# A planned attention and GLU kernel: half-gate Tanh kept in its partitions, |Q| of the first heads by a VectorE bit mask, and another table of scheduling rules

## The chip, the core and the metric

The kernel runs on one core of a Trainium2 chip. The metric is device time in microseconds (us) of one execution; lower is better. In the profile PE is TensorE, ACT is ScalarE, DVE is VectorE, POOL is GpSimd, and SP is the SyncE queue that issues nearly all DMAs. PSUM is the memory that matmuls write; a bank of it holds 128 partitions x 512 float32 values.

## The reference, cut to what matters

Everything is bfloat16 at the borders, with S = 2048 tokens, D = 640, H = 32 heads of Dh = 20, and F = 1728.

```python
xn = layernorm(x)
q, k, v = split(xn @ wqkv)                    # 32 heads of 20
p = softmax(q @ k.T * 20 ** -0.5)             # 2048 x 2048 per head
s = (p @ v) @ wo
h = sigmoid(xn @ w_gate) * (xn @ w_up)        # 2048 x 1728
g = silu(h @ w_down)
out = x + s * g
```

The heaviest part is the softmax: 32 heads x 2048 x 2048 exponentials.

## The kernel before

**Tiles.** Four heads form a group, 512 queries form a chunk: 8 groups x 4 chunks make 32 blocks. A block has 64 score tiles (4 heads x 16 key tiles), each 128 keys x 512 queries, made by one matmul (`score_mm`, L931). There are 2048 score tiles in all.

**Two ways to an exponential.** A score tile goes one of two ways. On ACT an Exp turns it into bfloat16 (`pt`, all through the helper at L142): two tiles at once, 128 x 1024, from a PSUM pair `scA`, and sometimes a third tile, 128 x 512, from a single bank `bk`. On DVE the tile is read out of a bank as int16 (`iv`, L1310), and four such tiles together go through three more passes (`passes`: L1019, L1022 and L1025) that build the exponential from the bits (`pb`). PE then multiplies `pt` and `pb` by V and sums the result in one bank (L967).

**A bound on the scores.** Instead of a running maximum the kernel subtracts a bound. For it the absolute value of Q is needed in bfloat16. For the first two groups (heads 0 to 7, `mk_q`) five matmuls make Q in a bank, ACT writes `aq` = |Q| (`q_abs`, L232), one matmul adds the bound to the same bank (L236), and DVE writes `q` (L239). The first block does this in the prologue, so seven such items are left for the main part. For the other heads (`mk_qu`) Q goes to SBUF first, and DVE makes |Q| there by masking the sign bit (L611).

**The GLU.** The sigmoid is computed as Tanh: h is made as (1 + tanh(g/2)) * u, and the halves are made good later. For each chunk of 512 tokens there are 13 full tiles of 128 hidden columns: gate matmuls, Tanh on ACT to `tnh`, up matmuls, and one DVE instruction (L716) to `hT`. The last 64 hidden columns share one matmul output: the gate is in partitions 0 to 63, the up part in partitions 64 to 127 (`mm2`, L720). There `th2` writes the Tanh of partitions 0 to 63 to partitions 64 to 127 of `tnh`, and `ev2` (L728) multiplies it with the up part and writes partitions 0 to 63 of `hT`. There are four such half tiles, one per chunk. The down projection follows (`mk_down`, L746), with a Tanh of its own on ACT (`td`) and a DVE instruction at L762; its result goes to DRAM (`gq_dram`) and comes back later.

**The end.** In the last eight blocks the output projection (`mk_out`, L805) is made tile by tile: DVE multiplies it with the gate (`otmp`, L812), POOL adds x (L815), SP stores the tile (L817). A tile of x and of the gate is loaded by `load_out` (L787, L788) into one of two places, so tile t can be loaded only after tile t-2 is done with its place.

**What sets the order.** The order of PE, ACT and DVE is not left to a scheduler of the compiler. The kernel contains a planner: while it builds the program it steps through an imagined time of its own, with a cost for each operation (for example 0.60 us for a DVE read of a bank), and at each step emits the next instruction of an engine that it holds to be free. On PE it chooses between filling score tiles (`F`), multiplying by V (`PV`) and the other matmuls (`M`). ACT takes fills in turn, DVE takes bank reads, passes and the items above. On the chip each engine runs its list in order, and semaphores keep the data right; the planner's time then has no meaning.

**The table.** The planner's choices hang on some 18 numbers, and `PLAN` has a row of them for each of the 32 blocks; a row comes into force when its block is begun (L1188). Among them are `s0` and `s1` (how far ahead DVE may be given score tiles), `rounds` (how many products with V must be ready), `mfew` (how many banks other items may take), `third`, `excl` and `lag`. The constant `D_LAST` (20) in `claim_dve` says with how many tiles left a block gives DVE no more of them:

```python
if n_left[b] >= (D_LAST if b < NBLK - 1 else D_LAST_END):
    js = [j for j in range(GH) if left[b][j] and j not in not_j]
    return take(b, max(js, key=lambda j: (j not in had, len(left[b][j]), j)), -1) if js else None
```

Of the kernel before, what the change touches and what calls it, by code (L numbers as in the profile page):

```python
# [11 lines left out]
BF16 = mybir.dt.bfloat16  # L12
I16 = mybir.dt.int16
ACT = mybir.ActivationFunctionType
ALU = mybir.AluOpType
# [3 lines left out]
P = 128  # L19
# [5 lines left out]
QC = 512  # L25
# [3 lines left out]
UC = UH * DH  # L29

B_PV = (3, 2, 1, 0)
LEAD, D_LAST, D_LAST_END, M_END = 40.0, 20, 8, 0.6
NPT, NPB, NIV = (21, 7), 4, 3
A_BANKS = (((), ()), ((0,), (1,)), ((0, 1, 2, 3), (1, 0, 2, 3)))
D_BANKS = ((2, 1, 0, 3), (2, 0, 1, 3), (0, 1, 2, 3), (1, 2, 0, 3))
M_BANKS = ((3, 2, 1, 0), (2, 3, 0, 1), (3, 1, 2, 0), (3, 0, 2, 1))

RULE = dict(urgent=0.25, rounds=4, hold=0.15, slack=0.2, s0=0.2, s1=0.2, wait3=0.4, fall=1, lag=0.0,
            dmax=2, third=2, dord=0, mord=0, mfew=2, npv=4, held=48, burst=1, excl=1)
KEYS = tuple(RULE)  # L40
PLAN = (
    (0.25, 4, 0.3, 0.2, 0.2, 0.2, 0.4, 1, 0.0, 2, 0, 0, 2, 2, 4, 48, 1, 1),
    (0.25, 4, 0.3, 0.2, 0.2, 0.5, 0.4, 1, 0.0, 2, 0, 0, 1, 2, 3, 48, 1, 1),
    (0.25, 4, 0.15, 0.2, 0.5, 0.2, 0.4, 1, 0.0, 2, 2, 0, 0, 2, 4, 48, 1, 1),
    (0.25, 2, 0, 0.2, 0.2, 0.5, 0, 1, 0.0, 2, 2, 0, 0, 2, 4, 48, 1, 1),
    (0.25, 4, 0.15, 0.2, 0.8, 0.2, 0.4, 1, 0.0, 2, 2, 0, 0, 2, 4, 40, 1, 1),
    (0.25, 4, 0.15, 0.2, 0.8, 1.2, 0.4, 1, 0.0, 2, 2, 0, 0, 1, 4, 40, 1, 1),
    (0.25, 4, 0.15, 0.5, 0.8, 1.2, 0.4, 1, 0.0, 2, 2, 0, 3, 1, 4, 32, 1, 1),
    (0.25, 2, 0.15, 0.5, 0.8, 0.8, 0.4, 1, 0.0, 2, 2, 0, 3, 1, 4, 32, 1, 1),
    (0.25, 2, 0.15, 0.5, 0.5, 0.8, 0.4, 1, 0.0, 2, 2, 0, 2, 1, 4, 32, 0, 1),  # L50
    (0.25, 2, 0.15, 0.5, 0.5, 0.8, 0.4, 1, 0.0, 2, 2, 0, 2, 1, 4, 32, 0, 1),
    (0.25, 2, 0.15, 0.5, 0.5, 1.2, 0.4, 1, 4.0, 2, 2, 0, 2, 1, 4, 56, 0, 1),
    (0.3, 2, 0.15, 0.5, 0.5, 1.2, 0.4, 1, 4.0, 2, 2, 3, 2, 1, 4, 56, 0, 1),
    (0.25, 4, 0.15, 0.2, 0.2, 0.8, 0.4, 1, 0.0, 2, 2, 0, 0, 1, 4, 64, 1, 1),
    (0.25, 4, 0.15, 0.2, 0.2, 1.2, 0.4, 1, 0.0, 2, 2, 0, 0, 2, 4, 48, 1, 1),
    (0.25, 4, 0.3, 0, 0.2, 1.2, 0.2, 1, 0.0, 2, 2, 0, 0, 2, 4, 48, 1, 1),
    (0.25, 4, 0.3, 0, 0.8, 1.2, 0.2, 1, 0.0, 2, 2, 0, 0, 2, 4, 48, 1, 1),
    (0.25, 4, 0.3, 0, 0.5, 1.2, 0.2, 1, 0.0, 2, 2, 0, 0, 1, 4, 48, 1, 1),
    (0.25, 4, 0.15, 0.2, 0.8, 0.2, 0.4, 1, 0.0, 2, 2, 2, 1, 2, 4, 48, 1, 1),
    (0.25, 4, 0.15, 0.2, 0.8, 0.2, 0.4, 1, 0.0, 2, 2, 2, 1, 2, 4, 48, 1, 1),  # L60
    (0.25, 4, 0.15, 0.2, 0.35, 0.2, 0.4, 1, 14.0, 2, 2, 0, 0, 2, 4, 48, 1, 1),
    (0.2, 4, 0.15, 0.2, 0.2, 0.8, 0.7, 1, 0.0, 2, 2, 0, 0, 2, 4, 48, 0, 1),
    (0.2, 4, 0.15, 0.2, 0.5, 0.8, 0.7, 1, 0.0, 2, 2, 0, 0, 2, 4, 48, 0, 1),
    (0.2, 4, 0, 0.2, 0.5, 0.8, 0.7, 1, 0.0, 2, 2, 0, 0, 2, 4, 48, 1, 1),
    (0.25, 4, 0.3, 0.5, 0.2, 1.2, 0.4, 1, 2.0, 2, 2, 0, 0, 2, 4, 48, 1, 1),
    (0.25, 4, 0.15, 0.2, 0.5, 0.2, 0.4, 1, 0.0, 2, 0, 2, 0, 2, 4, 48, 1, 1),
    (0.25, 4, 0.15, 0.2, 0.5, 0.8, 0.4, 1, 0.0, 2, 0, 2, 0, 2, 4, 32, 1, 1),
    (0.25, 4, 0.15, 0.2, 0.5, 0.2, 0.4, 1, 0.0, 2, 0, 2, 0, 2, 3, 32, 1, 1),
    (0.25, 7, 0.15, 0.2, 0.2, 0.2, 0.2, 1, 0.0, 2, 2, 0, 0, 2, 4, 48, 1, 1),
    (0.2, 7, 0.15, 0.2, 0.2, 0.2, 0.2, 1, 0.0, 2, 2, 0, 0, 2, 4, 48, 1, 1),  # L70
    (0.2, 7, 0.15, 0.2, 0.2, 1.2, 0.2, 1, 0.0, 2, 2, 0, 0, 2, 4, 48, 1, 1),
    (0.2, 7, 0.15, 0.2, 0.2, 0.5, 0.2, 1, 0.0, 2, 2, 0, 0, 2, 4, 48, 1, 1),
    (0.25, 4, 0.15, 0, 0.2, 0, 0.4, 1, 8.0, 2, 2, 0, 0, 2, 3, 48, 1, 1),
)

PRO = (
# [35 lines left out]
def kernel(  # L112
# [11 lines left out]
    nc = tc.nc  # L124
# [14 lines left out]
    def act_imm(o, i, func, scale):  # L139
        zero = mybir.ImmediateValue(dtype=FP32, value=0.0)  # L140
        sc = mybir.ImmediateValue(dtype=FP32, value=scale)
        return nc.scalar.add_instruction(mybir.InstActivation(  # L142
            func=func, name=nc.get_next_instruction_name(), engine=ENG.Activation,
            ins=[nc.scalar.lower_ap(i), zero, sc, zero], outs=[nc.scalar.lower_ap(o)]))
# [7 lines left out]
    wk = ctx.enter_context(tc.tile_pool(name="wk", bufs=2))  # L152
# [77 lines left out]
    def q_abs(ps):  # L230
        aq = wk.tile([P, QC], BF16, tag="aq", bufs=4, name="aq")
        nc.scalar.activation(out=aq, in_=ps, func=ACT.Abs)  # L232
        return aq
# [188 lines left out]
    hT = late.tile([P, NFT, QC], BF16, name="hT")  # L422
# [55 lines left out]
    NBLK = NG * NQC  # L478
# [18 lines left out]
    def mark(*e):  # L497
        return lambda t: ev_at.__setitem__(e, t)
# [33 lines left out]
    def mk_q(b, at):  # L532
        g, c = gc(b)
        st = {}

        def alloc():
            st["ps"] = misc_ps()

        def mm(kd):
            nc.tensor.matmul(st["ps"], lhsT=wslice(g, 0, kd), rhs=xnT[:, c, kd, :],  # L540
                             start=(kd == 0), stop=(kd == KD - 1))

        def ab():
            st["aq"] = q_abs(st["ps"])

        def ev():
            q_evac(st["ps"], qts[b % 3])
        return Item([("PE", alloc, [(T_MM, lambda kd=kd: mm(kd)) for kd in range(KD)]),
                     ("ACT", 0.48, ab),
                     ("PE", None, [(T_MM, lambda: q_bound(st["ps"], g, st["aq"]))]),  # L550
                     ("DVE", 0.60, ev, "free", lambda t: q_at.__setitem__(b, t))], at, pre=[("md", g)])

# [136 lines left out]
    def mk_gu(c, kf, at):  # L689
        st = {}  # L690
        fs = fsz[kf]
        k2, ko = divmod(kf, 2)

        def alloc0():
            if (c, k2) not in wgu_tiles:
                load_wgu(c, k2)
            st["g"] = misc_ps()

        def alloc1():
            st["u"] = misc_ps()  # L700
            if ko == 0:
                n = c * NK2 + k2 + 1
                if n < NQC * NK2:
                    load_wgu(*divmod(n, NK2))

        def mm(key, i, kd):
            w = wgu_tiles[(c, k2)]
            nc.tensor.matmul(st[key][0:fs, :], lhsT=w[:, i, kd, ko * P:ko * P + fs],  # L708
                             rhs=xnT[:, c, kd, :], start=(kd == 0), stop=(kd == KD - 1))

        def th():
            st["t"] = w2.tile([P, QC], BF16, tag="tnh", bufs=2, name="tnh")
            act_imm(st["t"][0:fs, :], st["g"][0:fs, :], ACT.Tanh, 0.5)

        def ev():
            nc.vector.scalar_tensor_tensor(out=hT[0:fs, kf, :], in0=st["t"][0:fs, :], scalar=1.0,  # L716
                                           in1=st["u"][0:fs, :], op0=ALU.add, op1=ALU.mult)

        def mm2(kd):
            nc.tensor.matmul(st["g"], lhsT=wgu_tiles[(c, k2)][:, 0, kd, P:2 * P],  # L720
                             rhs=xnT[:, c, kd, :], start=(kd == 0), stop=(kd == KD - 1))

        def th2():
            st["t"] = w2.tile([P, QC], BF16, tag="tnh", bufs=2, name="tnh")
            act_imm(st["t"][fs:P, :], st["g"][0:fs, :], ACT.Tanh, 0.5)

        def ev2():
            nc.vector.scalar_tensor_tensor(out=hT[0:fs, kf, :], in0=st["t"][fs:P, :], scalar=1.0,  # L728
                                           in1=st["g"][fs:P, :], op0=ALU.add, op1=ALU.mult)
        if fs < P:  # L730
            return [Item([("PE", alloc0, [(T_MM, lambda kd=kd: mm2(kd)) for kd in range(KD)]),
                          ("ACT", 0.48, th2), ("DVE", 0.60, ev2, "free", mark("h", c, kf))], at)]
        return [Item([("PE", alloc0, [(T_MM, lambda kd=kd: mm("g", 0, kd)) for kd in range(KD)]),
                      ("ACT", 0.48, th, "free", mark("t", c, kf))], at),
                Item([("PE", alloc1, [(T_MM, lambda kd=kd: mm("u", 1, kd)) for kd in range(KD)]),
                      ("DVE", 0.60, ev, "free", mark("h", c, kf))], at, gates={1: [("t", c, kf)]})]
# [124 lines left out]
    for b in range(NBLK):  # L861
        g, c = gc(b)
# [58 lines left out]
    def claim_dve(had, not_j):  # L921
        for b in range(base(), min(NBLK, base() + 2)):
            if q_at.get(b, 1e9) > now:
                return None
            if n_left[b] >= (D_LAST if b < NBLK - 1 else D_LAST_END):
                js = [j for j in range(GH) if left[b][j] and j not in not_j]
                return take(b, max(js, key=lambda j: (j not in had, len(left[b][j]), j)), -1) if js else None
        return None
# [592 lines left out]
```

## Time and profile before

| what | value |
|---|---|
| median of 6 runs | 812.03 us (808.84 to 812.68) |
| the profiled execution | 811.98 us |
| its span, first to last instruction | 810.3 us |
| granted TensorE clock, mean | 0.992 |
| busy in the span: ACT, DVE, PE | 782.2, 774.2, 769.1 us |
| first Exp of a score tile starts | 29.55 us |
| last Exp of a score tile ends | 792.97 us |

The busy time is the union of an engine's records. The record of an ACT or DVE instruction begins when the engine takes it up, which can be while the one before is still running; so records overlap, and the distance of two ends tells what an instruction costs in a full queue. In the tables of groups each line has the source line, the engine, the operation, output<-input with shapes, the count, then busy us and mean ns of one, then the engine's idle time before it and what ended it.

### The profile page before, as it was taken

How to read it: one execution, taken by the hardware profiler on the slowest of the kernel's cores; microseconds unless marked ns; L12 is line 12 of the kernel's file. 1: busy time of each engine (PE TensorE's matmuls, PEld its weight loads, DVE VectorE, ACT ScalarE, POOL GpSimd, SP SyncE). 2: the span in 40 equal slices, each digit the busy share in tenths (PEclk: the TensorE clock that was granted, in tenths of full speed). 3: DMA queues.
4: the chain of work that ended last, by engine and by line, in shares of the span. 5: the costliest groups of instructions: out<-in, count | busy, mean ns of one | idle time of the engine just before them, and what ended most of it. 6: DMA issues, size and time to landing. Idle time of an engine off the chain costs nothing.

```text
span 810.3 us, 17151 instructions
## 1 busy us (share of the span) xinstructions
PE 769.1 (95%) x6464; PEld 278.3 (34%) x6516; DVE 774.2 (96%) x1274; ACT 782.2 (97%) x1003; POOL 88.4 (11%) x107
## 2 busy tenths in 40 slices
PE   6899999999999999999999999999999999899985
PEld 5522333333333333334333333334332223333332
DVE  8899999999999999999999999999999999899986
ACT  8899999999999999999999999999999999999992
POOL 7000000010000000000000000000000001212135
PEclk9999999999999999999999999999999999999998
DMA  6611231223122223131112323432122323322431
GB/s 166 174 47 51 64 81 32 79 54 77 52 72 72 61 65 95 51 89 50 56 48 68 96 60 80 121 112 75 48 69 71 85 57 83 114 82 57 141 91 45
DMA packets 95875, 62.61 MB, mean 77 GB/s; under 512 B 36388, under 2 KB 89684, under 8 KB 95792
## 3 DMA queue, kind: packets, MB, share of 16 engines
q1 hardware_dynamic: 95504, 61.18, 27.0%
q8 instruction: 51, 0.84, 0.4%
q10 hardware_dynamic: 288, 0.33, 0.1%
q14 instruction: 32, 0.26, 0.1%
HBM read 47.84 MB, written 13.55 MB: 76 GB/s over the span
## 4 chain that ended last, share of the span: by engine, by line
ACT 57%; PE 25%; DVE 10%; issue 5%; DMA 2%; POOL 1%; SPq 0%; DVEq 0%; ACTq 0%; POOLq 0%
ACT pt L142 51%; PE scA L931 7%; PE bk L708 5%; PE bk L746 5%; PE bk L967 4%; DVE iv L1310 4%; ACT tnh L142 2%; DVE pb L1025 2%; ACT td L142 1%; PE bk L676 1%; POOL xnT L815 1%; DVE pb L1019 1%; DVE pb L1022 1%; ACT sq L338 1%; ACT xnT L362 1%
## 5 line engine op out<-in xcount | busy, mean ns | idle before, releaser
L142 ACT ACTIVATE pt<-scA 128x1024 bf16<-128x1024 f32 x698 | 711.6, 1222 | 3.0 <-PE bk L931 2.7
L1310 DVE TENSOR_SCALAR iv<-bk 128x512 int16<-128x512 f32 x499 | 330.5, 682 | 9.7 <-PE bk L931 7.5
L931 PE MATMUL scA<-q,kT 32*128 32x512 bf16 x1391 | 271.8, 382 | 16.8 <-ACT pt L142 12.6
L931 PE MATMUL bk<-q,kT 32*128 32x512 bf16 x657 | 200.1, 384 | 2.1 <-DVE otmp L812 1.9
L967 PE MATMUL bk<-pt,v 128*21 128x512 bf16 x1549 | 182.6, 382 | 0.0
L931 PEld LDWEIGHTS <-kT 32*128 32x128 bf16 x2048 | 88.1, 91 | 262.8 <-issue 249.7
L967 PE MATMUL bk<-pb,v 128*21 128x512 bf16 x998 | 157.2, 382 | 0.5 <-DVE pb L1025 0.4
L1025 DVE TENSOR_TENSOR pb<-iv,pb 128x2048 bf16<-128x2048 bf16 (+1 forms) x125 | 152.4, 1219 | 0.4
L708 PE MATMUL bk<-xnT,wgu 128*128 128x512 bf16 x488 | 138.4, 382 | 2.3 <-issue 1.3
L142 ACT ACTIVATE pt<-bk 128x512 bf16<-128x512 f32 x158 | 124.6, 789 | 3.2 <-PE bk L931 3.1
L1004 POOL TENSOR_TENSOR on_bf<-on,rl 128x512 bf16<-128x512 f32 x31 | 40.5, 1305 | 646.6 <-DVE rl L1002 581.4
L1019 DVE TENSOR_SCALAR pb<-iv 128x2048 int16<-128x2048 int16 (+1 forms) x125 | 86.8, 694 | 0.4
L1022 DVE TENSOR_SCALAR pb<-iv 128x2048 int16<-128x2048 int16 (+1 forms) x125 | 86.8, 695 | 0.0
L746 PE MATMUL bk<-wd,hT 128*128 128x320 bf16 x448 | 86.2, 306 | 0.6 <-ACT pt L142 0.4
L967 PEld LDWEIGHTS <-v 128*21 128x21 bf16 x2547 | 48.2, 90 | 88.2 <-issue 70.4
L708 PEld LDWEIGHTS <-wgu 128*128 128x128 bf16 x520 | 38.3, 97 | 60.6 <-issue 38.5
L746 PEld LDWEIGHTS <-hT 128*128 128x128 bf16 x448 | 36.4, 98 | 44.8 <-issue 34.7
L568 PE MATMUL bk<-xnT,wu 128*128 128x512 bf16 x151 | 44.4, 382 | 1.4 <-issue 0.5
L142 ACT ACTIVATE tnh<-bk 128x512 bf16<-128x512 f32 (+1 forms) x56 | 44.6, 796 | 0.1
L716 DVE SCALAR_TENSOR_TENSOR hT<-tnh,bk 128x512 bf16<-128x512 bf16 x52 | 35.5, 682 | 2.6 <-ACT tnh L142 0.9
L815 POOL TENSOR_TENSOR xnT<-otmp,xnT 128x320 bf16<-128x320 f32 x24 | 21.9, 924 | 59.6 <-DVE otmp L812 46.9
L676 PE MATMUL bk<-wv,xnT 128*128 128x160 bf16 x280 | 26.6, 234 | 0.2 <-issue 0.2
(116 smaller groups left out, 390.9 us busy)
## 6 DMA issues: line engine op xcount, KB each, us to landing
rl<-rd SPq DMA_DIRECT2D x124, 64.0 KB
wgu<-in_B_w_gate_dram SPq DMA_DIRECT2D x24, 320.0 KB
wgu<-in_B_w_up_dram SPq DMA_DIRECT2D x24, 320.0 KB
gq_dram<-gqs SPq DMA_DIRECT2D x24, 160.0 KB
xnT<-gq_dram SPq DMA_DIRECT2D x12, 320.0 KB
xt<-in_A_x_dram SPq DMA_DIRECT2D x16, 160.0 KB
oD<-on_bf SPq DMA_DIRECT2D x120, 20.0 KB
wd<-in_B_w_down_dram SPq DMA_DIRECT2D x1, 2080.0 KB
```

The lines of the kernel that those rows point to most:

```text
L142: return nc.scalar.add_instruction(mybir.InstActivation(func=func, name=nc.get_next_instruction_name(), engine=ENG.Activation, ins=[nc.sca ...
L568: nc.tensor.matmul(st["ps"], lhsT=wus[u][:, kd, i, :], rhs=xnT[:, c, kd, :], start=(kd == 0), stop=(kd == KD - 1))
L708: nc.tensor.matmul(st[key][0:fs, :], lhsT=w[:, i, kd, ko * P:ko * P + fs], rhs=xnT[:, c, kd, :], start=(kd == 0), stop=(kd == KD - 1))
L716: nc.vector.scalar_tensor_tensor(out=hT[0:fs, kf, :], in0=st["t"][0:fs, :], scalar=1.0, in1=st["u"][0:fs, :], op0=ALU.add, op1=ALU.mult)
L746: nc.tensor.matmul(st["ps"][:, 0:HD], lhsT=hT[0:fsz[kf], kf, t4 * P:(t4 + 1) * P], rhs=wd[0:fsz[kf], kf, h * HD:(h + 1) * HD], start=(kf = ...
L931: nc.tensor.matmul(dst, lhsT=kTs[gc(b)[0] % 2][32 * j:32 * j + 32, kt * P:(kt + 1) * P], rhs=qts[b % 3][32 * j:32 * j + 32, :], start=True ...
L967: nc.tensor.matmul(bank[pv_bank[0]][32 * j:32 * j + DH + 1, :], lhsT=lhsT, rhs=u["src"], start=first, stop=last, tile_position=(0, 32 * j) ...
L1004: nc.gpsimd.tensor_tensor(out=on_bf, in0=on, in1=rl, op=ALU.mult)
L1019: nc.vector.tensor_scalar(out=pb[:, 0, :, :].bitcast(I16), in0=iv, scalar1=0x7F80, scalar2=1, op0=ALU.bitwise_and, op1=ALU.bitwise_or)
L1022: nc.vector.tensor_scalar(out=pb[:, 1, :, :].bitcast(I16), in0=iv, scalar1=0x007F, scalar2=0x3F00, op0=ALU.bitwise_and, op1=ALU.bitwise_or)
L1025: nc.vector.tensor_tensor(out=pb[:, 1, :, :], in0=iv.bitcast(BF16), in1=pb[:, 1, :, :], op=ALU.mult)
L1310: nc.vector.tensor_scalar(out=d["iv"][:, j, :], in0=bank[bk], scalar1=B_OFF, scalar2=0.0, op0=ALU.add, op1=ALU.max)
```

## The change

It has three parts. First, `th2` writes the Tanh of the half gate tile to partitions 0 to 63, where its input lies, and `ev2` reads it from there; its planned cost goes from 0.60 to 0.75. Second, |Q| in `mk_q` is no longer an Abs on ACT: DVE reads the high 16 bits of each float32 in the bank and masks the sign bit. The first block's Abs in the prologue stays on ACT. Third, all rows of `PLAN` are other ones, and the two thresholds of `claim_dve` become columns of the table.

```diff
-LEAD, D_LAST, D_LAST_END, M_END = 40.0, 20, 8, 0.6
+LEAD, M_END = 40.0, 0.6
...
-            dmax=2, third=2, dord=0, mord=0, mfew=2, npv=4, held=48, burst=1, excl=1)
+            dmax=2, third=2, dord=0, mord=0, mfew=2, npv=4, held=48, burst=1, excl=1, dl=20, dle=8)
 KEYS = tuple(RULE)
 PLAN = (
-    (0.25, 4, 0.3, 0.2, 0.2, 0.2, 0.4, 1, 0.0, 2, 0, 0, 2, 2, 4, 48, 1, 1),
-    (0.25, 4, 0.3, 0.2, 0.2, 0.5, 0.4, 1, 0.0, 2, 0, 0, 1, 2, 3, 48, 1, 1),
...
+    (0.25, 4, 0.15, 0.2, 0.8, 0.2, 0.4, 1, 0.0, 2, 2, 0, 0, 2, 4, 48, 0, 1, 20, 8),
+    (0.25, 5, 0.3, 0.2, 0.8, 0.2, 0.4, 1, 0.0, 2, 2, 0, 0, 3, 4, 48, 0, 1, 20, 8),
...
         def ab():
-            st["aq"] = q_abs(st["ps"])
+            st["aq"] = wk.tile([P, QC], BF16, tag="aq", bufs=4, name="aq")
+            high = st["ps"].bitcast(I16).rearrange("p (q h) -> p q h", h=2)[:, :, 1]
+            nc.vector.tensor_scalar(out=st["aq"].bitcast(I16), in0=high, scalar1=0x7FFF, scalar2=0,
+                                    op0=ALU.bitwise_and, op1=ALU.bitwise_or)
...
-                     ("ACT", 0.48, ab),
+                     ("DVE", 0.60, ab),
...
         def th2():
             st["t"] = w2.tile([P, QC], BF16, tag="tnh", bufs=2, name="tnh")
-            act_imm(st["t"][fs:P, :], st["g"][0:fs, :], ACT.Tanh, 0.5)
+            act_imm(st["t"][0:fs, :], st["g"][0:fs, :], ACT.Tanh, 0.5)
 
         def ev2():
-            nc.vector.scalar_tensor_tensor(out=hT[0:fs, kf, :], in0=st["t"][fs:P, :], scalar=1.0,
+            nc.vector.scalar_tensor_tensor(out=hT[0:fs, kf, :], in0=st["t"][0:fs, :], scalar=1.0,
                                            in1=st["g"][fs:P, :], op0=ALU.add, op1=ALU.mult)
...
-                          ("ACT", 0.48, th2), ("DVE", 0.60, ev2, "free", mark("h", c, kf))], at)]
+                          ("ACT", 0.48, th2), ("DVE", 0.75, ev2, "free", mark("h", c, kf))], at)]
...
-            if n_left[b] >= (D_LAST if b < NBLK - 1 else D_LAST_END):
+            if n_left[b] >= (rule["dl"] if b < NBLK - 1 else rule["dle"]):
```

In the instruction order of the changed program the numbers of instructions differ as follows; all other instructions are as many as before, in another order.

| instruction | before | changed |
|---|---|---|
| ACT Exp, 128 x 1024 from `scA` | 693 | 686 |
| ACT Exp, 128 x 512 from `bk` | 158 | 179 |
| ACT Exp, 128 x 512 from `scA` | 5 | 0 |
| ACT Abs, main part | 7 | 0 |
| DVE bit mask from a bank | 0 | 7 |
| DVE `iv`, 128 x 512 | 499 | 497 |
| DVE passes of a last, smaller group (two masks, one product) | 3 of 1536 columns | 3 of 512 columns |
| add of x to an output tile: POOL / DVE | 24 / 0 | 23 / 1 |
| changes of PE between fills, PV and other matmuls | 1428 | 1367 |

## The prediction

> **What bounds the kernel now.** I read the busy shares, then the busy time by stretch, then the tables of groups by shape, then the timeline of ACT and DVE where a stretch shows idle time.
>
> ```profile
> PE 769.1 (95%) x6464; PEld 278.3 (34%) x6516; DVE 774.2 (96%) x1274; ACT 782.2 (97%) x1003; POOL 88.4 (11%) x107
> ...
> 50.00:700.00 650.00, 630.88 (x5254) 215.21 (x5294) 635.80 (x1026) 649.70 (x815) 36.98 (x30) 1.00 0.25 69
> 700.00:716.00 16.00, 14.33 (x104) 5.61 (x102) 12.33 (x22) 13.31 (x19) 6.08 (x6) 0.89 0.55 171
> 775.00:793.00 18.00, 17.14 (x148) 6.47 (x146) 14.60 (x24) 16.27 (x22) 9.13 (x10) 0.94 0.34 102
> ```
>
> After the stretch and its length come PE, weight loads, DVE, ACT and POOL. Three engines look alike in the first line, but from 50 to 700 us ACT is busy 649.70 of 650 us, DVE 635.80. A full record can still hide a wait, because ACT's records overlap, so I looked at their ends:
>
> ```profile
> 522.60 1.35 ACT L142 ACTIVATE pt<-scA 128x1024 bf16<-128x1024 f32 x1
> 523.97 0.59 ACT L142 ACTIVATE tnh<-bk 64x512 bf16<-64x512 f32 x1
> 524.58 2.86 ACT L142 ACTIVATE pt<-scA 128x1024 bf16<-128x1024 f32 x3
> ...
> 685.41 0.60 ACT L142 ACTIVATE pt<-bk 128x512 bf16<-128x512 f32 x1
> 685.90 1.94 ACT L142 ACTIVATE pt<-scA 128x1024 bf16<-128x1024 f32 x2
> ```
>
> The three Exp from 524.58 take 2.86 us; the first, started on an empty engine, takes 1.025 (the line at 708.90 further down is such a one, 1.02), so the next two end (2.86 - 1.025)/2 = 0.917 us apart. At 685.41 a single tile is followed by the next start after 0.49. So in a full queue a 1024-wide Exp costs 0.917 and a 512-wide one 0.490: 0.427 per 512 columns and 0.063 fixed, which makes 0.330 of a 320-wide `td`. The half Tanh at 523.97 starts only when the one before has ended (522.60 + 1.35 = 523.95) and the next starts only when it has ended: end to end 0.61 instead of 0.490, and the next Exp ends 1.05 later instead of 0.917. It costs 0.744 in all.
>
> ```profile
> L142 ACT ACTIVATE pt<-scA 128x1024 bf16<-128x1024 f32 x693 | 709.2, 1225 | 3.0 <-PE bk L931 2.7
> L142 ACT ACTIVATE pt<-bk 128x512 bf16<-128x512 f32 x158 | 124.6, 789 | 3.2 <-PE bk L931 3.1
> L142 ACT ACTIVATE tnh<-bk 128x512 bf16<-128x512 f32 x52 | 42.2, 812 | 0.0
> L232 ACT ACTIVATE aq<-bk 128x512 bf16<-128x512 f32 x7 | 5.5, 791 | 0.0
> L239 DVE TENSOR_SCALAR q<-bk 128x512 bf16<-128x512 f32 x7 | 4.8, 687 | 0.1
> L611 DVE TENSOR_SCALAR aq<-qu 120x512 int16<-120x512 int16 x16 | 4.5, 282 | 0.0
> L728 DVE SCALAR_TENSOR_TENSOR hT<-tnh,bk 64x512 bf16<-64x512 bf16 x4 | 2.8, 690 | 0.6 <-ACT tnh L142 0.3
> ```
>
> ACT's work in the main part: 693 x 0.917 + (158 + 52 + 7 + 5) x 0.490 + 4 x 0.744 + 32 x 0.330 = 635.5 + 108.8 + 3.0 + 10.6 = 757.9 us. From the first Exp (29.55) to the end of the last (792.97) are 763.4 us. So 5.5 us are waiting, and ACT is the bound: 99.3% filled. About 3.1 of the 5.5 lie at 708 to 716, some 2.1 after 775:
>
> ```profile
> 708.41 0.60 ACT L142 ACTIVATE pt<-bk 128x512 bf16<-128x512 f32 x1 [1.55 <-PE bk L931]
> 708.90 1.02 ACT L142 ACTIVATE pt<-scA 128x1024 bf16<-128x1024 f32 x1
> ...
> 706.52 0.89 DVE L812 SCALAR_TENSOR_TENSOR otmp<-bk,xnT 128x320 f32<-128x320 f32 x2 [2.34 <-DMA xnT<-gq_dram]
> ...
> 787.03 1.88 DVE L1310 TENSOR_SCALAR iv<-bk 128x512 int16<-128x512 f32 x3
> ```
>
> At 706.52 DVE stood 2.34 us for a reloaded gate tile; PE then lacked a bank and ACT a fill. The line at 787.03 gives DVE's price: (1.88 - 0.68)/2 = 0.60 per bank read.
>
> **The change part by part.** *Half Tanh.* Writing to its own partitions, ACT has the shape of any 512-wide Tanh: 4 x (0.744 - 0.490) = -1.0 us. For `ev2` the row is L728: 690 ns, and in the timeline it neither overlaps the one before nor the one after. The Trainium skill (VectorE: DVE Perf Modes, "Two Vector instructions with no wait between them") says that an instruction is held until all before have ended when an input starts in another 32-partition quadrant than the last read from that memory. That agrees, and speaks against a gain on DVE: the up part still starts at partition 64 of PSUM, so `ev2` stays held. I take no change; bounds -0.12 x 4 and +0.06 x 4, all on DVE.
>
> *|Q|.* ACT loses 7 x 0.490 = -3.4 us. DVE gains seven masks. By operation the nearest row is L611, 282 ns; by what it reads it is L239, a bank, 687 ns, 0.60 in a queue. The skill's same page ("Why PSUM operands drop a tier") allows a PSUM source two results a cycle at best, and ("What auto-detection actually checks") that needs 16-bit data with step 1; here the step is 2. So 7 x 0.60 = 4.2 us; by L611 it would be about 2. The mask also puts a wait into DVE's queue: for the five Q matmuls, with bank reads queued behind it, and the bound matmul waits for it. The items are made a block ahead (763/32 = 24 us), which hides this; without that cover it is about 7 x 0.6 = 4 us.
>
> *The table: ACT against DVE.* The counts: ACT -7 of 1024, +21 of 512 from banks, -5 of 512 from `scA`: -6.4 + 10.3 - 2.5 = +1.4 us (two tiles more, nine instructions more). ACT in all: -1.0 - 3.4 + 1.4 = -3.0 us, to 754.9. DVE: +4.2, two bank reads less -1.2, the last group's passes narrower. Their rows are 548, 547 and 959 ns at 1536 columns and 696, 695 and 1221 at 2048, so 512 columns should cost about 254, 254 and 435: -1.1. One add moves from POOL (about 0.5, from the 481 ns of L812). In all DVE +2.4. It had 14 us without a record in 50 to 700 alone, so this is not on the path.
>
> *The table: the order.* PE changes 1367 times between kinds of work instead of 1428, with the same matmuls but two; PE is not the bound. Whether ACT keeps filled is what the trace before can't show. Sorting both orders into the work of PE between two fills: over 1.6 us it is 16 times before and 20 times after, largest 1.97 and 2.73 us, against 0.92 to 1.41 us of Exp in one fill and another waiting. That is much alike; I give +0.4 for the one large gap. Before the last fills there is no run of eleven output matmuls any more, where ACT stood 1.2 us at 777: -1.2. Behind the last DVE pass one more `otmp` is left: +0.4. SP issues the same loads and stores. They stand in another order where tiles are reloaded, which is the first rival below. Bounds of the order alone: -5.5 (no wait left) and +10 (below).
>
> Sum: -3.0 + 0.4 - 1.2 + 0.4 = -3.4 us on the profiled 811.98 (span 810.3 and 1.7 around it): 808.6. The median, 812.03, is the same within 0.05.
>
> **The rivals.** *Slower: the reload of output tiles.* DVE's work between freeing a place and using it again is 7.2, 3.6, 27, 28, 12.6, 4.7, 24, 22, 3.8 and 4.1 us before, for tiles 2 to 11; after it is 4.1, 6.6, 36, 39, 4.1, 3.8, 21, 23, 8.4 and 5.6. At 3.6 DVE stood 2.34 us and ACT lost 3.1; there SP issued the load only at 703.4, behind four stores of `oD`, a load of `lt` and a store of `out` that held SP for 1.32 us. At 3.8, 4.1 and 4.7 no load was waited for. After the change three stand at 4.1, 4.1 and 3.8. If all three meet a full SP queue: 3 x 3.1 - 3.1 = +6.2, with -3.0 and the tail's +0.4 about 816. It turns slower once two of three wait like that. For: the place is known to stall. Against: one in four did. I give all such ways 0.22.
>
> *The gain is given back.* DVE's share is less even: summing the larger of ACT's, DVE's and PE's work over groups of four blocks gives 777 before and 779 after, where ACT fell by 3. Where DVE leads (the second to fourth blocks: 73.6 us against ACT's 71.1), ACT waits later than before: about +3, so 811.5. Chance 0.16. That the mask costs more than 0.60 ends here too.
>
> *The waits close too.* If the order leaves about 1.5 of 5.5 us of waits: 804.5. Chance 0.14.
>
> **How the numbers follow.** The forecast has 0.48, and its own range is 806.5 to 810.5. A measurement of this kernel tells about 0.3%, 2.4 us, from no change, so faster means under 809.6 and slower over 814.5. Faster: 0.14 and 0.46 of the forecast's, 0.60; within: 0.02 and 0.16, 0.18; slower 0.22. The range 804.0 to 815.5 leaves out about 0.1 at each end.
>
> **What would show it.** Right: ACT from first to last Exp about 760 us with 50 to 700 still full; `tnh` 64x512 without a gap before it and no Exp held behind it; `aq` on DVE at about 0.68 us a record. Wrong: idle ACT released by PE scores after `otmp` waits for `gq_dram`; gaps on ACT where DVE leads; `aq` well over 0.7 us; a first Exp that starts elsewhere than 29.5.

## The result, and the profile after

| | before | changed |
|---|---|---|
| median | 810.11 us (72 runs, 808.45 to 813.25) | 808.13 us (34 runs, 805.91 to 810.96) |
| ratio to before, 95% interval | | 0.9972 (0.9965 to 0.9980) |
| the profiled execution | 811.98 us | 806.70 us |
| its span; granted clock, mean | 810.3 us; 0.992 | 805.0 us; 0.983 |
| first Exp starts, last Exp ends | 29.55, 792.97 us | 30.20, 788.52 us |

The change made the kernel faster by 0.28%, 2.3 us. Measured again beside the experiments, the gain was 0.12% (0.01 to 0.24), so its size is not known well. The six runs of before that the forecast started from were high: with 72 the median is 810.11. So the two profiled executions differ by more (5.3 us) than the medians (2.0): the one of before was 1.9 above its median, the one of the changed kernel 1.4 below. Sizes of single terms are read from the traces in what follows, the worth of a change from the ratios.

The busy shares of the changed kernel and its busy time by stretch (after the stretch and its length: PE, weight loads, DVE, ACT and POOL with their counts, then granted clock, DMA share and GB/s):

```profile
PE 761.7 (95%) x6458; PEld 274.1 (34%) x6514; DVE 778.1 (97%) x1280; ACT 777.7 (97%) x1005; POOL 90.7 (11%) x106
...
50.00:700.00 650.00, 631.80 (x5350) 219.12 (x5397) 639.43 (x1034) 649.46 (x832) 38.31 (x30) 1.00 0.25 70
700.00:716.00 16.00, 15.88 (x139) 5.56 (x139) 15.97 (x29) 15.54 (x18) 4.36 (x5) 1.00 0.53 160
716.00:735.00 19.00, 14.89 (x116) 3.71 (x119) 17.10 (x27) 17.69 (x21) 1.26 (x1) 0.73 0.11 32
...
750.00:766.00 16.00, 13.17 (x96) 3.00 (x95) 14.67 (x23) 14.12 (x16) 5.31 (x5) 0.68 0.55 169
```

ACT is still the bound: 649.46 of 650 us from 50 to 700. DVE grew from 774.2 to 778.1 while ACT fell from 782.2 to 777.7. What is new stands at the end: from 716 to 735 and from 750 to 766 the granted clock is 0.73 and 0.68, ACT has 1.3 and 1.9 us without work, and PE is *less* busy than elsewhere. The groups that the change touches, by shape (count, then busy us and mean ns of one, then idle time before):

```profile
L142 ACT ACTIVATE pt<-scA 128x1024 bf16<-128x1024 f32 x686 | 709.4, 1224 | 5.7 <-PE bk L934 3.4 <-PE scA L934 2.2
L142 ACT ACTIVATE pt<-bk 128x512 bf16<-128x512 f32 x179 | 143.6, 802 | 0.0
L546 DVE TENSOR_SCALAR aq<-bk 128x512 int16<-128x512 int16 x7 | 4.8, 686 | 0.1
L731 DVE SCALAR_TENSOR_TENSOR hT<-tnh,bk 64x512 bf16<-64x512 bf16 x4 | 2.8, 690 | 0.1
L142 ACT ACTIVATE tnh<-bk 64x512 bf16<-64x512 f32 x4 | 2.4, 607 | 0.0
```

The mask takes 686 ns a record, the price of a bank read as forecast, not the 282 of the mask from SBUF. `ev2` keeps its 690 ns.

Three places hold nearly all of ACT's waits. The first, in the timeline (start, duration, engine, line; in brackets the idle time before and what ended it), is the reload of an output tile:

```profile
698.32 0.49 DVE L815 SCALAR_TENSOR_TENSOR otmp<-bk,xnT 128x320 f32<-128x320 f32 x1 [1.10 <-DMA xnT<-gq_dram]
...
698.87 0.37 PE L934 MATMUL bk<-q,kT 32*128 32x512 bf16 x1 [0.79 <-DVE otmp L815]
...
700.46 1.94 ACT L142 ACTIVATE pt<-scA 128x1024 bf16<-128x1024 f32 x2 [0.99 <-PE scA L934]
```

DVE stands 1.10 us for the gate tile, PE then 0.79 for a bank, ACT 0.99 for a fill. The second place is this:

```profile
722.36 0.39 PE L934 MATMUL scA<-q,kT 32*128 32x512 bf16 x2 [0.52 <-ACT pt L142]
...
723.27 0.61 PE L934 MATMUL scA<-q,kT 32*128 32x512 bf16 x2 [0.53 <-ACT pt L142]
...
729.42 1.25 PE L808 MATMUL bk<-xnT,v 128*128 128x320 bf16 x4
...
730.59 0.61 PE L934 MATMUL scA<-q,kT 32*128 32x512 bf16 x2
...
731.30 1.02 ACT L142 ACTIVATE pt<-scA 128x1024 bf16<-128x1024 f32 x1 [0.75 <-PE scA L934]
...
732.75 4.07 ACT L142 ACTIVATE pt<-scA 128x1024 bf16<-128x1024 f32 x4 [0.42 <-PE bk L934]
```

From 719.6 on PE has little but fills: a pair of score matmuls of 0.39 us, then 0.53 us idle until ACT frees the next pair of banks. At 723.27 the same pair takes 0.61: the granted clock had fallen to half at 722.9, and it stayed so for 10.2 us, to 733.2. The fills themselves are still in time. But at 729.42 the other work comes back, four output matmuls take 1.25 us at this clock, the next fill starts at 730.59, and ACT waits. The third place, 759 to 764, is of the same kind: the clock was half from 753.7 to 763.9, and ACT stood 0.44, 0.48 and 0.91 us for score tiles.

Adding up by how much two ends lie further apart than the prices allow, all waits over 80 ns make 5.0 us, where before had 5.8: 1.1 by the reload, 3.9 in the two stretches of half clock. In before the clock was half only for 3.4 us from 708.8 and 3.4 us from 773.7 (an expectation below gives these places as 703 and 768, which is some 6 us too early). Behind the last Exp it is halved in both kernels.

### The profile page after: what moved, and what is told of

Its sections match the earlier page's. It is cut to its first block, busy times and chain, and to the rows that moved or that the text cites. A ratio compares the mean times of both kernels' runs of the same rounds, so it can differ in the third digit from the quotient of the medians.

```text
span 805.0 us, 17176 instructions
## 1 busy us (share of the span) xinstructions
PE 761.7 (95%) x6458; PEld 274.1 (34%) x6514; DVE 778.1 (97%) x1280; ACT 777.7 (97%) x1005; POOL 90.7 (11%) x106
## 4 chain that ended last, share of the span: by engine, by line
ACT 67%; PE 21%; DVE 5%; issue 5%; DMA 1%; POOL 1%; SPq 0%; ACTq 0%; DVEq 0%; POOLq 0%
ACT pt L142 61%; PE scA L934 7%; PE bk L749 5%; PE bk L970 5%; ACT tnh L142 4%; PE bk L711 1%; DVE iv L1313 1%; ACT td L142 1%; PE bk L808 1%; DVE pb L1028 1%; DVE xn L350 0%; ACT xnT L362 0%; PE bk L934 0%; DVE pb L1025 0%; PE bk L841 0%
## 5 line engine op out<-in xcount | busy, mean ns | idle before, releaser
L934 PE MATMUL bk<-q,kT 32*128 32x512 bf16 x676 | 208.3, 387 | 1.3 <-DVE otmp L815 0.8
L934 PEld LDWEIGHTS <-kT 32*128 32x128 bf16 x2048 | 85.4, 91 | 266.3 <-issue 254.8
L970 PE MATMUL bk<-pt,v 128*21 128x512 bf16 x1551 | 175.2, 386 | 0.1
L970 PE MATMUL bk<-pb,v 128*21 128x512 bf16 x994 | 149.5, 386 | 0.0
L142 ACT ACTIVATE pt<-bk 128x512 bf16<-128x512 f32 x179 | 143.6, 802 | 0.0
L749 PE MATMUL bk<-wd,hT 128*128 128x320 bf16 x448 | 84.3, 302 | 0.1
L818 POOL TENSOR_TENSOR xnT<-otmp,xnT 128x320 bf16<-128x320 f32 x23 | 24.2, 1070 | 57.6 <-DVE otmp L815 53.7
```

Of the source, the lines that this page charges most:

```text
L142: return nc.scalar.add_instruction(mybir.InstActivation(func=func, name=nc.get_next_instruction_name(), engine=ENG.Activation, ins=[nc.sca ...
L749: nc.tensor.matmul(st["ps"][:, 0:HD], lhsT=hT[0:fsz[kf], kf, t4 * P:(t4 + 1) * P], rhs=wd[0:fsz[kf], kf, h * HD:(h + 1) * HD], start=(kf = ...
L934: nc.tensor.matmul(dst, lhsT=kTs[gc(b)[0] % 2][32 * j:32 * j + 32, kt * P:(kt + 1) * P], rhs=qts[b % 3][32 * j:32 * j + 32, :], start=True ...
L970: nc.tensor.matmul(bank[pv_bank[0]][32 * j:32 * j + DH + 1, :], lhsT=lhsT, rhs=u["src"], start=first, stop=last, tile_position=(0, 32 * j) ...
```

## The experiments

Before was run again beside each group of kernels, on the same chip, with medians from 809.9 to 810.9 us. All ratios are to it, that of the changed kernel to the 72 runs above. The distance is from the first Exp's start to the last Exp's end, and the waits are those over 80 ns, counted by ends; both are of the one profiled execution. "Dummies" are matmuls that nobody reads; their numbers are those in the program.

| kernel | median us | ratio (95%) | distance us | waits us |
|---|---|---|---|---|
| before | 810.1 | 1 | 763.4 | 5.8 |
| changed | 808.1 | 0.9972 (0.9965 to 0.9980) | 758.3 | 5.0 |
| changed, again | 809.7 | 0.9988 (0.9976 to 0.9999) | 760.3 | 7.0 |
| before + half Tanh | 808.5 | 0.9979 (0.9968 to 0.9991) | 759.2 | 4.0 |
| before + mask | 812.0 | 1.0017 (1.0005 to 1.0030) | 766.0 | 11.6 |
| changed, old table | 820.6 | 1.0128 (1.0107 to 1.0148) | 758.1 | 3.9 |
| before, new table | 823.8 | 1.0166 (1.0141 to 1.0191) | 765.2 | 5.4 |
| changed, half Tanh undone | 810.6 | 0.9993 (0.9980 to 1.0006) | 761.1 | 5.4 |
| changed, Abs on ACT again | 812.0 | 1.0017 (1.0005 to 1.0029) | 765.7 | 9.2 |
| changed + 113 dummies | 806.4 | 0.9961 (0.9948 to 0.9973) | 758.6 | 5.3 |
| before + 20 dummies | 811.1 | 1.0011 (1.0005 to 1.0018) | 761.8 | 4.1 |
| changed + 56 dummies | 806.9 | 0.9950 (0.9932 to 0.9968) | 756.0 | 2.8 |
| changed, no reload | 805.1 | 0.9936 (0.9919 to 0.9952) | 757.6 | 4.3 |
| changed, no reload, 56 dummies | 801.0 | 0.9885 (0.9868 to 0.9903) | 753.5 | 0.3 |

**The changed kernel again.**

> The changed kernel itself, for a comparison on the chip of this call: 0.997 of before, with half clock on PE for about 10 us after 722 and after 753.

809.68 us. The two long half clocks came as expected, for 10.2 us from 724.1 and 6.8 us from 758.2. A third was not expected: 3.4 us from 700.2, just behind the reload's wait. ACT waits 2.6 us there, at 701 to 704, where the first profile had 1.1 and full clock, and 0.5 at 437. DVE's wait for the gate tile is hardly longer (1.26 us against 1.10). So what follows the reload differs from execution to execution, and half clock goes with the longer waits.

**Half Tanh alone, and half Tanh undone.** In before, and the other way round in the changed kernel, with each engine's order as it was:

```diff
-            act_imm(st["t"][fs:P, :], st["g"][0:fs, :], ACT.Tanh, 0.5)
+            act_imm(st["t"][0:fs, :], st["g"][0:fs, :], ACT.Tanh, 0.5)
...
-            nc.vector.scalar_tensor_tensor(out=hT[0:fs, kf, :], in0=st["t"][fs:P, :], scalar=1.0,
+            nc.vector.scalar_tensor_tensor(out=hT[0:fs, kf, :], in0=st["t"][0:fs, :], scalar=1.0,
```

> The kernel before with the half Tanh alone: Tanh written to partitions 0 to 63 and read from there, the planned cost and so the order of every engine unchanged. Theory (ACT is the bound and its work sets the time): in the trace of the changed kernel a half Tanh ends 0.19 to 0.31 us after the one before instead of 0.61, and no Exp is held behind it, so ACT's first-to-last-Exp time falls by about 2.5 us and the run is 2 to 2.5 us faster. The forecast's own size was 1.0. Rival (it is given back, PE or DVE set the pace): within 0.5 us of before.

> The changed kernel with only the Tanh of the half tile put back into partitions 64 to 127, order identical. Theory (the half Tanh in its own partitions also clears the lag that the Exps before it have built up): +2 to +2.5 us, about 811.5. Rival (only the duration of the instruction, 0.744 against 0.49): +1.0 us, 810. Second rival (lost to waits later on): 0.

Alone in before it gave -1.7 us (-2.6 to -0.7). Undoing it cost 0.4 to 1.7 us, by which of the two measurements of the changed kernel it is set against. Both lie below the 2 to 2.5 us expected, and the times do not tell 1.0 from 2.0; the traces do. The timeline of ACT around one half tile, the changed kernel first, then the one with the half Tanh undone:

```profile
325.52 1.33 ACT L142 ACTIVATE pt<-scA 128x1024 bf16<-128x1024 f32 x1
326.42 0.61 ACT L142 ACTIVATE tnh<-bk 64x512 bf16<-64x512 f32 x1
326.90 1.96 ACT L142 ACTIVATE pt<-scA 128x1024 bf16<-128x1024 f32 x2
```

```profile
324.73 2.24 ACT L142 ACTIVATE pt<-scA 128x1024 bf16<-128x1024 f32 x2
326.99 0.59 ACT L142 ACTIVATE tnh<-bk 64x512 bf16<-64x512 f32 x1
327.60 1.94 ACT L142 ACTIVATE pt<-scA 128x1024 bf16<-128x1024 f32 x2
```

In the second the Exps end at 324.73 + 2.24 = 326.97 and the two behind the Tanh at 329.54: 2.57 us, two times 0.917 and 0.74 for the Tanh, the price that the prediction had taken. In the first these ends are 326.85 and 328.86: 2.01 us, which leaves 0.18 for the Tanh and not the 0.49 of a full tile. Counted so, the four half tiles of the changed kernel cost 0.29, 0.18, 0.27 and 0.19 us, and 0.74 each with the half Tanh undone. The four together are thus worth 2.0 us. The distances agree roughly: 761.1 against 758.3, with 0.4 more waits.

**The mask alone, and the mask undone.** Both kernels keep every engine's order; only the one instruction changes its engine.

```diff
-            st["aq"] = q_abs(st["ps"])
+            st["aq"] = wk.tile([P, QC], BF16, tag="aq", bufs=4, name="aq")
+            high = st["ps"].bitcast(I16).rearrange("p (q h) -> p q h", h=2)[:, :, 1]
+            nc.vector.tensor_scalar(out=st["aq"].bitcast(I16), in0=high, scalar1=0x7FFF, scalar2=0,
+                                    op0=ALU.bitwise_and, op1=ALU.bitwise_or)
```

> The kernel before with the absolute Q alone: the seven Abs of the main part become a DVE mask of the bank at the place where the planner put them, the order of all other instructions unchanged. Theory (ACT is the bound): ACT loses 7 x 0.490 = 3.4 us, DVE gains 7 x 0.60 in the first 182 us, where it has little free, so 2 to 3.4 us faster. Rival (DVE is as full as ACT there): bank reads queued behind the mask come late, ACT waits for fills, and the run is within 1 us of before.

> The changed kernel with its planned order kept, but the absolute value of heads 0 to 7 computed on ScalarE again in the mask's place (the plan still holds 0.60 us of VectorE for it). Theory (ScalarE is the bound, and the new order hides the mask): +3.4 us of ScalarE (7 x 0.49) and a little earlier banks, so +3 to +3.5 us, about 812.5. Rival (the mask costs as much as it saves, as it did in the old order, where it was +1.6 us): 0 to -1.6 us, 807 to 809.5.

In the old order the mask makes the kernel slower, by 1.4 us: ACT's waits rise from 5.8 to 11.6, more than the 3.4 us of Abs that are gone. About 4.5 of the 5.8 us lie before 205 us, where the masks are; most of the rest lies near 779, where the clock was half for 6.8 us in this execution and for 3.4 in that of before. The timeline of before with the mask shows one of the seven:

```profile
65.12 0.67 DVE L546 TENSOR_SCALAR aq<-bk 128x512 int16<-128x512 int16 x1
...
66.31 0.68 DVE L1313 TENSOR_SCALAR iv<-bk 128x512 int16<-128x512 f32 x1
...
67.04 0.81 PE L711 MATMUL bk<-xnT,wgu 128*128 128x512 bf16 x3 [0.58 <-DVE iv L1313]
...
68.27 3.01 ACT L142 ACTIVATE pt<-scA 128x1024 bf16<-128x1024 f32 x3 [0.73 <-PE scA L934]
```

DVE works without a pause; the bank read at 66.31 comes 0.6 us further behind the read before it than without the mask, PE stands 0.58 us for that bank, and 1.2 us later ACT stands 0.73 for a fill. In the new order the reverse holds: putting Abs back on ACT costs 2.3 to 3.6 us (1.0017 against 0.9988 and 0.9972), as ACT's 7 x 0.49 says. The profiled execution of that kernel, its slowest with 814.67 us, had half clock at a further place (704 to 711), with 3.9 of its 9.2 us of waits from 704 to 711. So the mask pays where the order was planned with it, and costs where it was put into an order planned without it. That this hangs on the new table is not shown: with the old table, planned anew with the mask (the next run), ACT was busy 174.95 of the 175 us from 30 to 205, against 171.47 with the mask in the old order.

**The tables exchanged.**

```diff
 PLAN = (
-    (0.25, 4, 0.15, 0.2, 0.8, 0.2, 0.4, 1, 0.0, 2, 2, 0, 0, 2, 4, 48, 0, 1, 20, 8),
+    (0.25, 4, 0.3, 0.2, 0.2, 0.2, 0.4, 1, 0.0, 2, 0, 0, 2, 2, 4, 48, 1, 1, 20, 8),
...
```

> The changed kernel with the rows of the old table (thresholds 20 and 8): both small parts, planned anew by the old rules. Its ACT work is 755.1 us by counts and prices, 2.7 less than before. Theory (ACT's work plus its waits): it is 2.7 us faster if its waits stay at 5.5 us; the waits are not known ahead. Rival (the table carries the gain): a table fitted to another stream of work gives many waits, over 5 us more, and the run is slower than before.

> The kernel before with the new table alone: half Tanh and Abs as before, planned by the new rows. Its ACT work is 759.9 us, 2.1 more than before. Theory: 2 us slower if its waits stay at 5.5, more if the table does not fit. Rival (the table carries the gain): faster than before by 2 us or more.

Each table with the other instructions is slower, by 10.4 and 13.4 us, though ACT's distance is as short as the changed kernel's in the first (758.1 us). Most of the time is lost behind the last Exp: 29.8 us there to the end of the span in the first and 26.6 in the second, where before has 17.3 and the changed kernel 16.5. The many waits that one expectation had did not come (3.9 and 5.4 us); neither expectation had the tail. A stretch of the chain of waits of the changed kernel with the old table (start, duration, what) shows with what:

```profile
793.27 2.63 DMA out_dram<-xnT
...
795.92 3.06 DMA xnT<-in_A_x_dram
...
800.01 1.11 PE bk L749 x7
```

Down projections and output tiles that the other order had done earlier were left over, and with ACT empty an output tile's store (2.63 us) and the next one's load into its place (3.06 us) lie on the path in full. So the table has no worth of its own that could be added to that of the parts.

**Dummy products against the half clock.** Where PE has nothing else in the last four blocks, a product of 256 columns goes into an idle bank and is read by nobody:

```diff
+        def keep_warm():
+            f = next((f for f in range(NFX) if flex[f] <= now), None)
+            if f is not None and warm_at[0] <= now:
+                nc.tensor.matmul(bank[f][:, 0:256], lhsT=ident, rhs=kTs[0][:, 0:256], start=True, stop=True,
+                                 skip_group_check=True)
+                warm_at[0] = now + 0.12
...
+            if free["PE"] <= now and NBLK - 4 <= base() and claimed[0] < NJOB * NBLK:
+                keep_warm()
```

> The changed kernel with 146 matmuls of 256 columns added in the last four blocks, into free banks and read by nothing, where PE has nothing but fills; the order of everything else is the same. Theory (the fill-only stretches let the granted clock fall to half, and the products with V that follow come late for ACT): the clock stays 1.0 from 716 to 766, the ACT waits at 731 to 734 and 759 to 764 (4.1 us together) are gone, and the run is 3 to 4 us faster than the changed kernel. Rival (PE is short of time there with full clock too, or the added matmuls delay fills): waits of about the same size and no gain, or slower.

> The kernel before with the same rule: 53 added matmuls in the last four blocks. Its half-clock windows at 703 and 768 us lasted 3.4 us each, and there the wait for a reloaded tile and a burst of eleven output matmuls stood nearby. Theory (the clock is a small part there): the window at 768 and the ACT wait of 1.2 us at 777 go, the one at 706 stays, about 1 us faster. Rival (the clock is the cause of both): 3 us faster or more.

The program has 113 dummies in the changed kernel and 20 in before, not the 146 and 53 expected. The changed kernel gained 0.27%, and the clock of its five runs was 0.996 to 0.997. But its distance of Exps was about the same, 758.6: with six dummies between two fills the Exps stood 1.08 us apart instead of 0.92. In before nothing was gained (1.0011). In its profiled execution the wait at 777 is gone and the reload's at 709 stayed, as the theory had it, and neither half clock is there. But none of the 20 dummies lies between 700 and 716, so the full clock there was not their work, and over all runs the mean clock is that of before without dummies, 0.994. This run thus says little on what the clock costs in before. The number of dummies was then cut to half, 56 (`now + 0.30` in place of `now + 0.12`):

> The changed kernel with small dummy products (256 columns, into an idle bank, read by nobody) on TensorE in the last four blocks where it has only fills, two for each fill where the run before with dummies had six (56 in all). Theory (clock): the lost time at 723 to 733 and 754 to 764 us is half clock after fill-only stretches; two dummies of 0.11 us beside a fill of 0.39 give 0.6 of each 0.92 us, enough to hold the clock at 1.0, and the fills start on time, so the Exps stay 0.92 us apart where six dummies made it 1.08 (8 x 0.165 + 7 x 0.165 = 2.5 us): about 804, 2 us under the six-dummy kernel and 4 to 5 under the changed one. Rival (ballast): what helped was not the clock, and the time is that of the changed kernel, 808 to 810; or the clock drops in spite of the dummies and the time is the same as that.

A row of its busy time by stretch:

```profile
716.00:735.00 19.00, 17.70 (x171) 6.71 (x170) 18.56 (x31) 19.00 (x23) 1.27 (x1) 1.00 0.12 33
```

The clock is 1.00, as it is from 750 to 766, and from 716 to 735 ACT is busy 19.00 of 19 us, where it was 17.69. Between two fills there stand mostly three dummies (0.50 us), not two, and the Exps are 0.92 us apart again. This is the fastest of nine executions. The median, 806.94 us over runs from 803.83 to 808.88, is 0.5% below before, and no lower than with 113 dummies (806.36). Three runs had a mean clock of 0.995 to 0.997 and took 803.8 to 804.8 us, as forecast; the other six had 0.989 to 0.994, so they must have had further half clock, and took 806.5 to 808.9. Set against the changed kernel the two intervals overlap by a hair. In the profiled execution, what was left was at 700 as ever, and here:

```profile
750.26 1.54 POOL L818 TENSOR_TENSOR xnT<-otmp,xnT 128x320 bf16<-128x320 f32 x2 [3.36 <-DMA xnT<-in_A_x_dram]
...
751.08 0.49 DVE L815 SCALAR_TENSOR_TENSOR otmp<-bk,xnT 128x320 f32<-128x320 f32 x1 [1.08 <-POOL xnT L818]
...
751.62 0.38 PE L1190 MATMUL bk<-kT,ident 128*128 128x256 bf16 x2 [0.68 <-DVE otmp L815]
...
752.42 4.69 ACT L142 ACTIVATE pt<-scA 128x1024 bf16<-128x1024 f32 x5 [0.30 <-PE scA L934]
```

POOL waits 3.36 us for x of the reloaded tile, DVE then 1.08 for POOL to give back a place for `otmp`, and everything on DVE behind it is late; at 758.05 ACT waits once more, 0.94 us. This is the reload again, by its other load.

**Without the reload**, with the clock as it falls and with the 56 dummies. The output tiles after the first two then use what the first two left in the buffers, so those rows of the output are wrong:

```diff
-        nc.sync.dma_start(out=out_tiles[tt][0], in_=x2[tt * P:(tt + 1) * P, :])
-        nc.sync.dma_start(out=out_tiles[tt][1], in_=gq_dram[tt * P:(tt + 1) * P, :])
+        for i, src in enumerate((x2, gq_dram) if tt < 2 else ()):
+            nc.sync.dma_start(out=out_tiles[tt][i], in_=src[tt * P:(tt + 1) * P, :])
```

> The changed kernel without the reloads of x and of the gate's product for the output tiles after the first two: the later tiles use what the first two left in the two buffers, so their output rows hold wrong values; everything else keeps its order. Theory (clock): of the waits left on ScalarE only the one at 700 us (1.1 us, VectorE behind the reload) is the reload's, the ones at 731 to 734 and 759 to 764 (4.0 us) are the half clock's: -1.0 us, about 808, and the trace still shows waits at 731 and 760. Rival (the reload bounds the end, through GpSimd's sum, which waits for x, and VectorE's scaled tile, which waits for GpSimd): all of them go, -4 to -5 us, about 804.5. By a second rival the reload's traffic is hidden anyway: 0.

> The same leaving out of the reloads, in the kernel with two dummy products beside each fill of the fill-only stretches. Theory: the 2.7 us of ScalarE's waits that the kernel with dummies still showed (1.2 at 700, 0.4 at 752, 1.05 at 758) go back to the reload, the last two through VectorE's wait of 1.1 us for GpSimd at 750, which waited for x: -2.5 us against that kernel, about 804, and 4 us under the same leaving out without dummies. Rival (the dummies themselves delay the fills): only the 1.2 at 700 goes, about 805.5.

A row of the busy time by stretch, without the reload first, then without the reload and with dummies:

```profile
750.00:766.00 16.00, 13.36 (x109) 2.93 (x106) 14.18 (x22) 14.24 (x17) 3.22 (x3) 0.68 0.27 85
```

```profile
750.00:766.00 16.00, 14.77 (x155) 5.25 (x154) 15.88 (x25) 16.00 (x20) 2.55 (x3) 1.00 0.26 78
```

In the traces each theory was right for its own place. Without the reload only the wait at 700 goes and those at 730 and 760 stay, with the clock at 0.68 as in the changed kernel: they are the clock's. With the clock kept as well, ACT is busy 16.00 of 16 us at 750 to 766, and after 441 us it waits nowhere up to the last Exp: 0.3 us of waits in all. Two causes thus account for all but 0.3 us of the waits in the changed kernel's first profile.

In time the reload is worth more than the theory had. Leaving it out gained 2.9 to 4.2 us on the two measurements of the changed kernel (0.9936 against 0.9972 and 0.9988), where the theory had 1.0 and the rival 4 to 5; with the dummies it gained 5.3 us (0.9885 against 0.9950), where the theory had 2.5. The edit takes away the waits for the loads, their traffic (62.6 MB became 57.7) and their places in SP's queue at once; which of these counts is open. The two causes are not independent. With the same 56 dummies the clock was 0.989 to 0.997 in the nine runs with the reload and 0.996 to 0.998 in the five without. So in many executions the reload brings half clock of its own, as behind its wait at 700 in the second profile of the changed kernel.

This is also what the scatter goes with. In the runs of before beside the experiments the mean time is 809.3 us at a mean clock of 0.997 (23 runs), 810.4 at 0.995 (34), 812.0 at 0.992 (22) and 813.1 at 0.990 (12). A stretch of 3.41 us at half clock takes 0.002 off the mean over 810 us, so each step is about one such stretch more (a longer one behind the last Exp counts too), and goes with some 1.1 to 1.6 us. Whether the stretch makes the time or a longer wait makes both, these numbers do not tell. The five runs without reload and with dummies lie within 1.3 us, the 34 of the changed kernel within 5.1.

## Why the prediction was right, point by point

Forecast were 808.6 us, -3.4 us or -0.42% on the profiled 811.98. Measured were 808.13 and -0.28% (-0.35 to -0.20), so the gain was a third smaller than forecast, and in the second measurement smaller yet. The median lay so near the number partly by luck: the start of the sum was 1.9 us above the median of before, and of the terms below one was too small, one had the wrong content and one the wrong sign.

- *ACT's counts: right.* Outside the half tiles the forecast was -3.4 + 1.4 = -2.0 us. The distance less the waits fell from 757.6 to 753.3, by 4.3 us: these 2.0, the 2.0 of the half tiles, and 0.3 left over. Abs put back on ACT cost 2.3 to 3.6 us.
- *The half Tanh: right mechanism, size wrong.* The step "4 x (0.744 - 0.490) = -1.0" held for its first price and not for the second: the traces show 0.74 and, on average, 0.23, so -2.0 us. The price of a full tile did not carry over.
- *`ev2` unchanged, mask at a bank read's price: right*, 690 and 686 ns.
- *"The items are made a block ahead, which hides this": wrong as a reason.* With exactly that lead, in the old order, the seven masks brought about 4.5 us more waits; the price "without cover", 4 us, was near. What waits is not the bound matmul but the bank reads behind the mask. DVE's 14 us without a record were no room, since only 3.1 of them lie from 30 to 205, where the masks are. An order planned with the mask made it free, with either table.
- *The order: the sum about right, its parts wrong.* The wait at 777 did go, as the absent run of eleven output matmuls said. But I set ACT's other waits as kept, and they were exchanged: 3.1 us at 708 became 1.1 at 700, and 3.9 us came through half clock, of which the forecast had nothing. Its own rows showed it, with a granted clock of 0.89 from 700 to 716 and 0.94 from 775 to 793. So the 3.1 us that it gave to the reload were not the reload's alone: in before with 20 dummies, where the clock stayed full there, 2.3 were left. The gaps of PE *work* between fills that I sorted say where PE is too full. What told here was where it is too empty: between 719.6 and 729 it has few products besides the fills.
- *The tail: +0.4 forecast, -0.8 found* (17.3 to 16.5 us), and the start was 0.65 later. Neither was tested.
- *The rivals.* The reload waits where it was sought, once, 1.1 us and not three times 3.1 in the first profile; but by the times without it, it is worth 2.9 to 4.2 us, and more again once the clock is kept. Uneven DVE gave nothing back that the trace would show: from 50 to 700 ACT is as full as before. The sum of "the waits close too" should have been 811.98 - 3.0 - 4.0 + 0.4, about 805.4 and not 804.5.

Not run: half Tanh and mask together in the old order. If their ratios simply add, 0.9979 and 1.0017 make no gain, and the new order carries the 2 us; that is an estimate.

## What to carry to other kernels

Where two engines are equally full, moving an instruction from one to the other gains only if the order is planned anew with it: the same mask was +1.4 us in the old order and -2.3 to -3.6 us in the new. When other work is moved out of a stretch so that only the matmuls that feed the bottleneck are left, look at the granted clock there; 56 idle products, mostly three between two fills, kept it there and left the fills on time, while six between two fills kept it and set the Exps 1.08 us apart; the medians of the two are alike. And look at more than one profiled execution, and at the granted clock of all runs, before pricing a reload: its place cost 1.1 us in one profile and 2.6, with half clock, in the next, and the fastest of nine executions is not the kernel's time.

## What the runs showed of the hardware

- The clock fell to half although PE never stood still for more than about half a microsecond: in the 3.41 us up to 722.93 it was busy 1.57 us, with pairs of fills 0.92 us apart and 0.53 us idle between them. It came back 10.2 us later, after the products had returned at 729. The Trainium skill (TensorE: Matmul & The Clock Gate, "What's actually happening") tells of the half clock "after ≥1 idle window (~3.4µs)"; this window was not idle, PE was busy 0.46 of the time. With mostly three dummies more between two fills (2.92 of 3.40 us busy) the clock stayed at 1.00. The traces show no sharp limit: it fell also after 2.40 busy us of 3.41 (750.24 to 753.65), and in before with the new table it stayed full after 1.90 of 3.40 (523.6 to 527.0). Up to the last Exp, the lengths of half clock in all traces here are 3.4, 6.8 and 10.2 us, multiples of 3.41, which agrees with the window of that page.
- In a full queue an Exp of 1024 columns starts 0.904 us after the one before but ends 0.917 after it, so the records grow, here from 1.02 to 1.33 us. A Tanh on 64 partitions that writes to its own partitions takes about 0.61 us, starts while the last Exp runs, and adds only 0.18 to 0.29 us; the record behind it is back at 1.01 to 1.07. That the gathered lag is what it saves is my reading. It fits the eight half tiles of the changed kernel and of before with the half Tanh: the Tanh ends 0.37 us after the Exp before it where that Exp's record took 1.13 us, 0.31 where it took 1.23, and 0.19 where it took 1.33 or 1.36. No run varied the lag alone. Written to the other 64 partitions the same Tanh overlaps neither neighbour and adds 0.74.
